# Whole 128x128 array tiles for the first queries' scores, their transposes and the last tokens' values

## The chip, the cores and the metric

One Trainium2 chip, of which the kernel uses one core. The time is the device time of one execution in microseconds (us), as the median of several runs; a profiled execution of the same kernel gives the trace from which all rows below come.

## The reference

Three stages follow each other on 4 sequences of 576 tokens. The first is windowed attention with 8 heads of 64 (each query sees itself and the 63 tokens before it). The second is a mixture of four causal attention experts with 64 channels each, of which each token takes the two with the largest gate. The third multiplies by cosines and sines of a projection, mixes tokens and channels and adds a rectified product. The change touches the second stage alone:

```
logits = x @ w_gate                      # gates: [token, 4]
for e in range(E):                       # E = 4 experts, Hd = 64
    q, k, v = x @ wq[e], x @ wk[e], x @ wv[e]
    scores = scale * (q @ k.transpose(0, 2, 1))
    scores = np.where(causal, -1000000000.0, scores)
    ...
    a /= a.sum(-1, keepdims=True) + 1e-09
    ye = a @ v @ wo[e]
    ...
```

## The kernel before, in words

All matrix products run on TensorE: a weight load puts a stationary operand of up to 128 rows and 128 columns into the array, and a matmul streams the moving operand past it. Where 32-bit precision is wanted, an operand is split into a high and a low part (`mm3`: three matmuls instead of one).

The work of the four images (the four sequences; `b` is 0 to 3) is cut into streams, which generator functions write: `phase_a` (windowed attention, matmuls of lines 288, 316, 156 and 159), `qk` (projections to queries and keys), `vg_gates` (projections to values and gates, four experts' values and the four gate columns side by side, 260 columns), `attn` (expert attention, in two passes `ep` of two experts each, thus 8 passes in all), `wo` (its output), and later `theta`, `mix` and `channel` for the third stage. `merge` interleaves the streams by costs written out by hand (the dictionary `KN`); the attention of one image runs beside the windowed attention and the projections of the next. A planner in the framework then sorts the instructions of each engine by when it estimates them to be ready, and sets the semaphores.

`vg_gates` goes over the tokens in five tiles: four of 128 and a last one of 64 (576 = 4 x 128 + 64). The tokens are the stationary operand, so the last tile loads 64 columns of weights. Line 384 copies the sums from PSUM to SBUF on ScalarE.

`attn` goes over the queries in five tiles of another cut: a first one of 64 queries (`t == 0`, `m = 64`), then four of 128. For each tile and each of the two experts, the scores are one or two pairs of matmuls (lines 460 and 462, queries stationary); VectorE adds the mask and takes the maximum (line 464), ScalarE the exponential (line 469), VectorE sums and inverts (lines 473 and 474), and GpSimd or VectorE scales by sum and gate (line 481). The scaling writes the diagonal block of both experts into the tile `pd`, of which two buffers take turns. TensorE transposes the other blocks (line 492) and the diagonal one (line 498, tile `bdt`); copies bring them back to SBUF (lines 494 to 502), and the products with the values follow (lines 156, 159 and 510), those of lines 156 and 159 in halves of 64 columns of the array, the second half from column 64 on. For the first tile, scores, transposes and copies have 64 queries: the scores load 64 columns of weights, the transpose has 64 rows of weights and an identity matrix of 64x64.

Of the kernel before, what the change touches and what calls it, by code (L numbers as in the profile page):

```python
# [21 lines left out]
P = 128  # L22
# [35 lines left out]
def kernel(ctx, tc, qT, kT, vw, consts, w_in, w_o, w_th, w_tk, w_ch, outT):  # L58
    nc = tc.nc
# [5 lines left out]
    ident, ma1, ma0 = (cst[:, P * i : P * i + P] for i in range(3))  # L65
# [17 lines left out]
    def bank(shape, tag, name):  # L83
        return ps.tile(shape, F32, tag=tag, bufs=BANKS[tag], name=name)

    def pool_mul(out, in_, by):
        nc.gpsimd.tensor_scalar(out=out, in0=in_, scalar1=by, scalar2=1.0,  # L87
                                op0=ALU.mult, op1=ALU.mult)
# [10 lines left out]
    def mm3(out, wh, wl, xh, xl, first, last):  # L99
        nc.tensor.matmul(out, wh, xh, start=first, stop=False)  # L100
        nc.tensor.matmul(out, wh, xl, start=False, stop=False)  # L101
        nc.tensor.matmul(out, wl, xh, start=False, stop=last)  # L102
# [96 lines left out]
    KL = [bp.tile([P, S], F32R, tag=f"KL{e}", name=f"KL{e}") for e in range(E)]  # L199
    for e in range(E):  # L200
        z = slice(64 - 64 * (e % 2), 128 - 64 * (e % 2))
# [172 lines left out]
    def vg_gates(b):  # L374
        xh, xl = X[b]
        vg = bp.tile([P, 5, E * D + E], F32, tag="vg", bufs=2, name=f"vg{b}")
        VG[b] = vg
        for i in range(5):
            w = min(P, S - i * P)
            g = bank([P, E * D + E], ("ggggg", ("as", "ta", "g", "as", "ta"), ("as", "ta", "as", "ta", "as"), ("bs", "tb", "bs", "tb", "bs"), ("bs", "g", "tb", "g", "bs"))[KN["VB"][b]][i], f"vg{b}{i}")  # L380
            for c in range(NC):
                mm3(g[:w], xh[:, c, i * P : i * P + w], xl[:, c, i * P : i * P + w],
                    wih[:, c, 2 * P : W0], wil[:, c, 2 * P : W0], c == 0, c == NC - 1)
            nc.scalar.copy(out=vg[:w, i, :], in_=g[:w])
            yield 1.3

        sh4 = [P, 5, E, E]
        lg = bp.tile([P, 5, E], F32, tag="lg", bufs=2, name=f"lg{b}")
        nc.gpsimd.memset(lg[64:128, 4, :], 0.0)
        pool_mul(lg[:, 0:4, :], vg[:, 0:4, E * D :], 1.0)  # L390
        pool_mul(lg[0:64, 4, :], vg[0:64, 4, E * D :], 1.0)
        mx = bp.tile([P, 5], F32, tag="gmx", name=f"gmx{b}")
        nc.vector.tensor_reduce(out=mx, in_=lg, op=ALU.max, axis=AX.X)
        ex = GX[:, :, :E]
        nc.vector.tensor_sub(out=ex, in0=lg, in1=mx.unsqueeze(2).to_broadcast([P, 5, E]))
        nc.scalar.activation(out=ex, in_=ex, func=AF.Exp)
        lf, lo = lg.unsqueeze(2).to_broadcast(sh4), lg.unsqueeze(3).to_broadcast(sh4)
        df = bp.tile(sh4, F32, tag="gle", name=f"gdf{b}")
        nc.vector.tensor_sub(out=df, in0=lf, in1=lo)
        gt = bp.tile(sh4, F32, tag="ggt", name=f"ggt{b}")  # L400
        nc.vector.scalar_tensor_tensor(out=gt, in0=df, scalar=0.0, in1=tie.unsqueeze(1).to_broadcast(sh4),
                                       op0=ALU.is_equal, op1=ALU.mult)
        nc.vector.scalar_tensor_tensor(out=gt, in0=df, scalar=0.0, in1=gt, op0=ALU.is_gt, op1=ALU.add)
        rk = bp.tile([P, 5, E], F32, tag="grk", name=f"grk{b}")
        nc.vector.tensor_reduce(out=rk, in_=gt, op=ALU.add, axis=AX.X)
        nc.vector.scalar_tensor_tensor(
            out=ex, in0=rk, scalar=1.5, in1=ex, op0=ALU.is_lt, op1=ALU.mult
        )
        sm = bp.tile([P, 5], F32, tag="gsm", name=f"gsm{b}")
        nc.vector.tensor_reduce(out=sm, in_=GX, op=ALU.add, axis=AX.X)  # L410
        nc.vector.reciprocal(out=sm, in_=sm)
        nc.vector.tensor_mul(out=ex, in0=ex, in1=sm.unsqueeze(2).to_broadcast([P, 5, E]))
        gw = bp.tile([P, 5, E], F32, tag="gw", bufs=2, name=f"gw{b}")
        nc.vector.tensor_copy(out=gw[64:128, 1:5, :], in_=ex[0:64, 1:5, :])
        nc.vector.tensor_copy(out=gw[0:64, 1:5, :], in_=ex[64:128, 0:4, :])
        last = nc.vector.tensor_copy(out=gw[0:64, 0, :], in_=ex[0:64, 0, :])
        if b == B - 1:
            gated[0] = last
        GW[b] = gw
# [3 lines left out]
    def sbank(b, shape, name):  # L423
        ns[0] += 1
        return bank(shape, "as" if b == B - 1 and ns[0] % KN["SB"] == 0 else "bs", name)

    def tbank(b, shape, name):
        nt[0] += 1
        return bank(shape, "ta" if b == B - 1 and nt[0] % KN["TB"] == 0 else "tb", name)

    def attn(b, ep):
        vg, gw = VG[b], GW[b]
        for i in range(2):
            e = 2 * ep + i
# [4 lines left out]
        for t in range(5):  # L439
            w = QW[t]  # L440
            q0 = 0 if t == 0 else 64 + P * (t - 1)
            m = 64 if t == 0 else P
# [5 lines left out]
            ss = sums(1, BS)  # L448
            sm = bp.tile([P, 2], F32, tag="bsm", bufs=4, name=f"bsm{b}{ep}{t}")
            pd = bp.tile([P, 2, 64], F32, tag="bpd", bufs=2, name=f"bpd{b}{ep}{t}")  # L450
            for i in range(2):
                e = 2 * ep + i
                n = f"{b}{e}{t}"
                qs, ka = QS[b, e], KA[b, e]
                ms = pn[:, i]
                cuts = [(0, w)] if w <= 512 else [(0, w // 2), (w // 2, w)]
                nm = bp.tile([P, 2], F32, tag="bnm", bufs=6, name=f"bnm{n}")
                for ci, (a, z) in enumerate(cuts):
                    s = sbank(b, [P, 512], f"bs{n}{a}")
                    nc.tensor.matmul(s[:m, : z - a], qs[:, q0 : q0 + m], ka[:, a:z],  # L460
                                     start=True, stop=False)
                    nc.tensor.matmul(s[:m, : z - a], qs[:, q0 : q0 + m], KL[e][:, a:z],  # L462
                                     start=False, stop=True)
                    nc.vector.tensor_tensor_reduce(  # L464
                        out=ms[:m, a:z], in0=s[:m, : z - a], in1=mb[:m, mo + a : mo + z],
                        scale=-0.125, scalar=nm[:m, 0:1] if ci else 3.0e38,
                        op0=ALU.add, op1=ALU.min, accum_out=nm[:m, ci : ci + 1],
                    )
                ex = nc.scalar.activation(out=ms[:m, :w], in_=ms[:m, :w], func=AF.Exp,  # L469
                                     bias=nm[:m, ci : ci + 1], scale=-1.0, accum_out=ss[:m, i, 0:1])  # L470
                if (b, ep, t, i) == (3, 1, KN["LT"], 1):
                    late[0] = ex
# [13 lines left out]
            for j0 in range(0, t, 2):  # L486
                jn = min(2, t - j0)
                pt = tbank(b, [P, 2, 2, P], f"bpt{b}{ep}{t}{j0}")
# [6 lines left out]
                else:  # L495
                    nc.scalar.copy(out=pT[:, j0 : j0 + jn], in_=pt[:, :jn])
            pt = tbank(b, [P, P], f"bdt{b}{ep}{t}")
            nc.tensor.transpose(pt[:, :m], pd[:m].rearrange("p h d -> p (h d)"), ident[:m, :m])
            if KN["BD"][b] == 0 or KN["BD"][b] == 1 and t % 2:
                nc.vector.tensor_copy(out=pT[:, t, 0, :m], in_=pt[:, :m])  # L500
            else:
# [2 lines left out]
            for f in together():  # L504
                for j in reversed(range(t)):
                    for i in range(2):
                        e = 2 * ep + i
# [383 lines left out]
    for i in range(2):  # L891
        nc.gpsimd.memset(VD[i][0:64, :, 1], 0.0)
        nc.gpsimd.memset(VD[i][64:128, :, 0], 0.0)
    merge((KN["QK"][8], qk(0, 0)), (KN["VG"][0], vg_gates(0)), (KN["PA"][6], phase_a(1, range(KN["AS"][1]))),
          (KN["CW"][5], load_w(w_in[:, W0:], NC, lambda c: wih[:, c, W0:], lambda c: wil[:, c, W0:], "bms")))
    for b in range(B):
        todo = [(KN["AT"][2 * b], attn(b, 0)), (KN["QK"][2 * b], qk(b, 1))]
        if KN["WOI"] == 2 * b:
            todo.append((KN["CW"][6], load_w(w_o, 2, lambda c: woh[c], lambda c: wol[c], "zc")))
# [16 lines left out]
        if b == 3:  # L916
# [4 lines left out]
            wkh += [kp.tile([P, S], F32R, name=f"wkh{c}") for c in range(NK0, 9)]  # L921
            wkl += [kp.tile([P, S], F32R, name=f"wkl{c}") for c in range(NK0, 9)]
        todo = [(KN["AT"][2 * b + 1], attn(b, 1))]
        if b < B - 1:
            todo += [(KN["QK"][2 * b + 1], qk(b + 1, 0)), (KN["VG"][b + 1], vg_gates(b + 1))]
# [100 lines left out]
```

## Time and profile before

| | before |
|---|---|
| median of 3 runs | 505.35 us (502.71 to 507.21) |
| profiled execution | 505.36 us |
| its span, first to last instruction | 503.6 us |
| TensorE's mean granted clock | 0.997 |
| busy: TensorE, VectorE, ScalarE, GpSimd | 480.2, 375.3, 343.4, 319.7 us |

In the rows, PE is TensorE's matmuls and PEld its weight loads, DVE is VectorE, ACT is ScalarE, POOL is GpSimd; L498 is line 498 of the kernel. A shape such as 64\*128 ahead of an operand is rows\*columns of the array. A matmul's recorded end is modelled and overlaps the next, so distances between starts say more than durations.

### The profile page before, as it was taken

What the parts mean: (1) busy time and instruction counts of PE and PEld (TensorE: products, weight loads), DVE (VectorE), ACT (ScalarE), POOL (GpSimd) and SP (SyncE); (2) the same over time, 40 slices, a digit from 0 to 9 for tenths busy, and PEclk for the clock granted to TensorE, in tenths of its full rate; (3) what the DMA queues carried; (4) which work ended last, traced back from release to release, by engine and by line L of the source; (5) the groups of instructions that cost most, each with busy time, mean ns of one, the idle gap of its engine ahead of it and who ended that gap; (6) DMA issues with size and microseconds to landing.
All of it is one profiled execution on the core that took longest, in us unless ns stands there. A gap on an engine that the chain in (4) does not pass through costs nothing.

```text
span 503.6 us, 12053 instructions
## 1 busy us (share of the span) xinstructions
PE 480.2 (95%) x4128; PEld 447.6 (89%) x4128; DVE 375.3 (75%) x1268; ACT 343.4 (68%) x1066; POOL 319.7 (63%) x406
## 2 busy tenths in 40 slices
PE   7899989999999999999999899999998999999997
PEld 5788978899998998989878788999998999999997
DVE  5857978776777858846898758987679938894942
ACT  7948778776877977869596698886177627652620
POOL 6758788772764861345595457679658926891770
PEclk9999998999999999999999999999999999999999
DMA  7574242430525242211146944231352044202002
GB/s 271 184 224 135 81 157 87 157 94 7 176 59 184 84 149 94 63 44 53 51 154 218 305 142 163 60 89 42 116 158 64 22 142 130 64 22 96 2 1 95
DMA packets 45614, 55.92 MB, mean 111 GB/s; under 512 B 6640, under 2 KB 34288, under 8 KB 45552
## 3 DMA queue, kind: packets, MB, share of 16 engines
q1 hardware_dynamic: 44688, 52.46, 32.9%
q10 hardware_dynamic: 864, 2.69, 1.6%
q8 instruction: 33, 0.54, 0.4%
q14 instruction: 29, 0.24, 0.2%
HBM read 43.34 MB, written 11.80 MB: 109 GB/s over the span
## 4 chain that ended last, share of the span: by engine, by line
PE 55%; DVE 19%; POOL 8%; ACT 7%; issue 6%; DMA 4%; SPq 0%; POOLq 0%; DVEq 0%; ACTq 0%
PE as L288 4%; PE c L100 3%; PE c L102 3%; PE apt L316 3%; PE c L101 3%; PE qk L100 3%; PE ao L159 2%; PE qk L102 2%; PE qk L101 2%; PE bs L460 2%; PE bpt L492 2%; PE vg L100 2%; ACT bms L469 2%; PE vg L102 2%; PE bs L462 2%
## 5 line engine op out<-in xcount | busy, mean ns | idle before, releaser
L311 POOL TENSOR_TENSOR ams<-ams,arc 128x384 f32<-128x384 f32 x48 | 39.8, 834 | 39.2 <-ACT ams L304 12.9
L304 ACT ACTIVATE ams<-ams,anm 128x128 f32<-128x128 f32 x144 | 56.5, 396 | 5.5 <-DVE anm L296 5.0
L469 ACT ACTIVATE bms<-bms,bnm 64x64 f32<-64x64 f32 (+4 forms) x80 | 44.8, 562 | 19.4 <-DVE bnm L464 17.9
L288 PE MATMUL as<-kt,QD 128*128 128x128 f32 x288 | 42.8, 286 | 2.1 <-DVE arc L309 0.7
L288 PEld LDWEIGHTS as<-kt,QD 128*128 128x128 f32 x288 | 37.1, 196 | 5.4 <-issue 2.0
L464 DVE CUSTOM_DVE_ANT_0 bms<-bs,mb 64x64 f32<-64x64 f32 (+4 forms) x80 | 32.3, 422 | 10.1 <-PE bs L462 6.0
L296 DVE CUSTOM_DVE_ANT_0 ams<-as,cst 128x128 f32<-128x128 f32 x144 | 34.5, 283 | 3.4 <-PE apt L316 2.1
L87 POOL TENSOR_SCALAR QD<-qt 64x576 f32<-64x576 f32 x24 | 31.0, 1290 | 8.6 <-DMA qt<-in_dram 4.1
L481 POOL TENSOR_SCALAR bpd<-bms,bsm,gw 128x64 f32<-128x64 f32 (+1 forms) x47 | 20.5, 437 | 22.9 <-DVE bsm L474 4.9
L97 POOL TENSOR_TENSOR cu<-x2T,cu 128x288 fp32r<-128x288 f32 x32 | 28.9, 916 | 8.0 <-ACT cu L94 8.0
L100 PE MATMUL y<-wkh,z 128*128 128x288 f32 x108 | 32.3, 302 | 0.1
L460 PE MATMUL bs<-KA,QS 128*128 128x288 f32 (+4 forms) x96 | 31.1, 333 | 1.0 <-DVE bnm L464 0.8
L101 PE MATMUL y<-wkl,z 128*128 128x288 f32 x108 | 32.0, 297 | 0.0
L102 PE MATMUL y<-wkh,z 128*128 128x288 f32 x108 | 31.3, 297 | 0.0
L660 ACT ACTIVATE ang<-th,magic 128x256 f32<-128x256 f32 x36 | 16.8, 469 | 20.5 <-PE th L102 20.0
L780 POOL TENSOR_TENSOR x2T<-x2T,u 128x288 f32<-128x288 f32 x20 | 16.6, 841 | 21.3 <-DVE u L791 11.1
L481 POOL TENSOR_SCALAR bms<-bms,bsm,gw 128x384 f32<-128x384 f32 (+3 forms) x40 | 26.7, 667 | 3.0 <-DVE bsm L474 3.0
L668 DVE TENSOR_TENSOR ang<-xk,ang 128x512 f32<-128x512 f32 x32 | 21.6, 683 | 8.8 <-ACT ang L665 5.7
L462 PE MATMUL bs<-KL,QS 128*128 128x288 f32 (+4 forms) x96 | 27.6, 297 | 0.0
L304 ACT ACTIVATION_READ_ACCUMULATOR ams<-ams,anm 128x1 f32 x144 | 27.6, 192 | 0.0
L316 PE MATMUL apt<-cst,ams 128*128 128x128 f32 x144 | 24.4, 277 | 3.3 <-ACT apv L321 2.1
L492 PE MATMUL bpt<-cst,bms 128*128 128x128 f32 x160 | 27.0, 278 | 0.2 <-DVE ol L97 0.2
(337 smaller groups left out, 2033.0 us busy)
## 6 DMA issues: line engine op xcount, KB each, us to landing
vt<-in_dram SPq DMA_DIRECT2D x48, 192.0 KB, 3.0
or<-od SPq DMA_DIRECT2D x32, 256.0 KB, 3.2
kt<-in_dram SPq DMA_DIRECT2D x15, 320.0 KB, 3.1
qt<-in_dram SPq DMA_DIRECT2D x16, 288.0 KB, 3.0
out_dram<-x2T SPq DMA_DIRECT2D x32, 144.0 KB, 1.8
w64k<-in_dram SPq DMA_DIRECT2D x5, 576.0 KB, 3.7
od<-oh SPq DMA_DIRECT2D x8, 288.0 KB, 2.1
od<-ol SPq DMA_DIRECT2D x8, 288.0 KB, 2.5
```

What stands on the lines that cost most here:

```text
L100: nc.tensor.matmul(out, wh, xh, start=first, stop=False)
L101: nc.tensor.matmul(out, wh, xl, start=False, stop=False)
L102: nc.tensor.matmul(out, wl, xh, start=False, stop=last)
L288: nc.tensor.matmul(s[:, i, :], qd[:, blk], kt[:, 64 * blk : 64 * blk + 128], start=True, stop=True)
L304: nc.scalar.activation(out=ms[:, i, :], in_=ms[:, i, :], func=AF.Exp, bias=nm[:, i : i + 1], scale=-1.0, accum_out=sm[:, i, 0:1],)
L311: nc.gpsimd.tensor_mul(out=ms, in0=ms, in1=rc.unsqueeze(2).to_broadcast([P, 3, P]))
L316: nc.tensor.transpose(pt[:, i, :], ms[:, i, :], ident)
L460: nc.tensor.matmul(s[:m, : z - a], qs[:, q0 : q0 + m], ka[:, a:z], start=True, stop=False)
L462: nc.tensor.matmul(s[:m, : z - a], qs[:, q0 : q0 + m], KL[e][:, a:z], start=False, stop=True)
L469: ex = nc.scalar.activation(out=ms[:m, :w], in_=ms[:m, :w], func=AF.Exp, bias=nm[:m, ci : ci + 1], scale=-1.0, accum_out=ss[:m, i, 0:1])
L481: eng.tensor_scalar(out=dst, in0=src, scalar1=sm[:m, i : i + 1], scalar2=gw[:m, t, 2 * ep + i : 2 * ep + i + 1], op0=ALU.mult, op1=ALU.mult)
L492: nc.tensor.transpose(pt[:, jj, i, :], pn[:, i, P * j : P * j + P], ident)
```

## The change

Three places that used a part of the array use all of it. The last tile of values and gates takes the last 128 tokens (64 of them a second time) and keeps the upper 64 partitions of the result. The scores of the first 64 queries load the first 128 queries; only the first 64 rows are read afterwards. The diagonal transpose of the first tile takes all 128 rows of `pd` and a 128x128 identity; rows 64 to 127 of `pd` are set to zero by GpSimd for it, ahead of the scores.

```diff
         for i in range(5):
             w = min(P, S - i * P)
...
+            tok = slice(i * P + w - P, i * P + w)
             for c in range(NC):
-                mm3(g[:w], xh[:, c, i * P : i * P + w], xl[:, c, i * P : i * P + w],
+                mm3(g, xh[:, c, tok], xl[:, c, tok],
                     wih[:, c, 2 * P : W0], wil[:, c, 2 * P : W0], c == 0, c == NC - 1)
-            nc.scalar.copy(out=vg[:w, i, :], in_=g[:w])
+            nc.scalar.copy(out=vg[:w, i, :], in_=g[P - w :])
...
             pd = bp.tile([P, 2, 64], F32, tag="bpd", bufs=2, name=f"bpd{b}{ep}{t}")
+            if m < P:
+                nc.gpsimd.memset(pd[m:], 0.0)
...
-                    nc.tensor.matmul(s[:m, : z - a], qs[:, q0 : q0 + m], ka[:, a:z],
+                    nc.tensor.matmul(s[:, : z - a], qs[:, q0 : q0 + P], ka[:, a:z],
                                      start=True, stop=False)
-                    nc.tensor.matmul(s[:m, : z - a], qs[:, q0 : q0 + m], KL[e][:, a:z],
+                    nc.tensor.matmul(s[:, : z - a], qs[:, q0 : q0 + P], KL[e][:, a:z],
                                      start=False, stop=True)
...
-            nc.tensor.transpose(pt[:, :m], pd[:m].rearrange("p h d -> p (h d)"), ident[:m, :m])
+            nc.tensor.transpose(pt, pd.rearrange("p h d -> p (h d)"), ident)
```

## Rows read from the trace of the kernel before

**Rows 1.** The page: busy time of the engines, and the chain's shares.
```profile
PE 480.2 (95%) x4128; PEld 447.6 (89%) x4128; DVE 375.3 (75%) x1268; ACT 343.4 (68%) x1066; POOL 319.7 (63%) x406
...
PE 55%; DVE 19%; POOL 8%; ACT 7%; issue 6%; DMA 4%; SPq 0%; POOLq 0%; DVEq 0%; ACTq 0%
```

**Rows 2.** Busy time by stage: length, then PE, PEld, DVE, ACT, POOL, clock, DMA.
```profile
45.00:240.00 195.00, 191.63 (x1867) 176.46 (x1866) 143.69 (x684) 151.10 (x544) 119.60 (x181) 0.99 0.31 100
240.00:303.00 63.00, 58.33 (x454) 50.88 (x453) 50.08 (x161) 48.28 (x134) 37.63 (x47) 1.00 0.54 174
```

**Rows 3.** Groups by line and shape, PE: count, busy us, mean ns, idle before.
```profile
L498 PE MATMUL bdt<-cst,bpd 64*128 64x64 f32 x8 | 2.2, 272 | 0.0
```

**Rows 4.** Instructions in order of time, PE, 191.0 to 192.1 us: start, duration.
```profile
191.06 0.31 PE L101 MATMUL x<-ol,woh 128*128 128x320 f32 x1
191.21 0.31 PE L102 MATMUL x<-oh,wol 128*128 128x320 f32 x1
191.45 0.27 PE L498 MATMUL bdt<-cst,bpd 64*128 64x64 f32 x1
191.65 0.40 PE L100 MATMUL qk<-x0h,wih 128*128 128x288 f32 x1
191.89 0.29 PE L101 MATMUL qk<-x0l,wih 128*128 128x288 f32 x1
192.02 0.29 PE L102 MATMUL qk<-x0h,wil 128*128 128x288 f32 x1
```

**Rows 5.** Instructions in order of time, PE, 152.1 to 152.2 us.
```profile
152.09 0.27 PE L498 MATMUL bdt<-cst,bpd 128*128 128x128 f32 x1
152.20 0.28 PE L288 MATMUL as<-kt,QD 128*128 128x128 f32 x1
```

**Rows 6.** The chain that ended last, 125.5 to 126.8 us: start, length.
```profile
125.72 0.59 PE ao L159 x21
126.31 0.20 PE bdt L498
126.51 0.34 PE x L100
```

**Rows 7.** Instructions in order of time, PE, 72.9 to 81.5 us.
```profile
72.94 0.29 PE L462 MATMUL bs<-KL,QS 128*128 128x288 f32 x1
73.07 0.19 PE L460 MATMUL bs<-KA,QS 128*64 128x64 f32 x1
...
81.40 0.27 PE L498 MATMUL bdt<-cst,bpd 128*128 128x128 f32 x1
```

**Rows 8.** Weight loads in order of time, PEld, 113.1 to 113.4 us.
```profile
113.18 0.14 PEld L460 LDWEIGHTS bs<-KA,QS 128*64 128x64 f32 x1
113.24 0.14 PEld L462 LDWEIGHTS bs<-KL,QS 128*64 128x64 f32 x1
113.30 0.19 PEld L288 LDWEIGHTS as<-kt,QD 128*128 128x128 f32 x1
```

**Rows 9.** Weight loads in order of time, PEld, 219.8 to 220.0 us.
```profile
219.80 0.19 PEld L462 LDWEIGHTS bs<-KL,QS 128*128 128x128 f32 x1
219.91 0.19 PEld L460 LDWEIGHTS bs<-KA,QS 128*128 128x128 f32 x1
```

**Rows 10.** Instructions in order of time, PE, 115.4 to 117.0 us.
```profile
115.41 0.28 PE L102 MATMUL vg<-wih,x1l 128*128 128x260 f32 x1
115.53 0.28 PE L100 MATMUL vg<-wih,x1h 128*64 128x260 f32 x1
...
116.94 0.27 PE L510 MATMUL o<-bpT,VD 128*128 128x128 f32 x1
```

**Rows 11.** Groups by line and shape, POOL, two memsets.
```profile
L389 POOL MEMSET lg<- 64x4 f32 x4 | 0.3, 97 | 0.2
L181 POOL MEMSET QD<- 64x192 f32 x1 | 0.3, 253 | 0.1
```

**Rows 12.** Groups by line and shape, ACT, the copies of line 384.
```profile
L384 ACT COPY vg<-vg 64x260 f32<-64x260 f32 x4 | 1.5, 367 | 1.0 <-PE vg L102 1.0
```

## The prediction

> **What bounds the kernel now.** Three views were read in this order: the page's summary and chain of waits, the busy time by stage, and the instructions of the touched places in order of time. The summary shows TensorE busy for 95% of the span, the next engine 75%, and the chain that ended last running over TensorE for 55% of the span, over VectorE for 19% and over GpSimd for 8% [rows 1]. The change lies in the attention stages, which end at about 303 us. From 45 to 240 us TensorE is busy 191.63 of 195.00 us: it hardly waits for anybody, so what it does there sets the pace. From 240 to 303 us, the last of the four images, it is busy 58.33 of 63.00 us and others set the pace for part of the time [rows 2]. A busy TensorE isn't one that works all the time, though: a stall shorter than the recorded tail of a matmul counts as busy. So the third view is read by starts: the time from one start to the next is what an instruction really costs, and the question is at which of the three edited places that distance is longer than it need be.
>
> **The diagonal transposes (8 of 40).** The first query tile has 64 rows, and its transposes use 64 rows of the array [rows 3]. In the example the last matmul ahead of one starts at 191.21 us and should take 0.15 us, as the one before it (191.06 to 191.21); the transpose starts only at 191.45, the next matmul 0.20 us later, and that one takes 0.24 us to its successor where the usual distance is 0.13 [rows 4]. From 191.21 to 192.02 are 0.81 us. A transpose that fills the array has no such gaps: from 152.09 to the next start are 0.11 us [rows 5]. With it the same stretch would be 0.15 + 0.11 + 0.13 + 0.13 = 0.52 us: 0.29 us less, although it streams twice the columns. So TensorE empties itself on the way into a 64-row tile and on the way out. I take six of the eight to be like this. The other two follow directly on the 64-column matmuls of line 159, which make the array empty itself anyway; there I estimate 0.10 us, the excess left on one side (0.24 less 0.13 in [rows 4]). The six of the first three images lie where TensorE sets the pace: 5 x 0.29 + 0.10 = 1.55 us. The two of the last image I count at nothing, because TensorE has 4.67 us of waits in that stage to lose them in. The chain agrees: it runs through five of the eight, 0.20 us each, as at 126.31 us [rows 6].
>
> **The first queries' scores (16 pairs of matmuls).** These load 64 columns of weights and stream 64. On the way in there is no gap: 72.94 to 73.07 us is 0.13, the usual distance of a matmul with 288 columns [rows 7]. Nor is there one within a run or on the way out: the weight loads start 0.06 us apart, and the next full load, of another kind of matmul, 0.06 us after the last of them [rows 8]. So no emptying is saved here. But with so little to stream the load is the limit, and a load of 128 columns for the next tile's scores takes 0.11 us from start to start [rows 9]. The change doubles each load: 0.05 us more. The first load of a pair hides beside the matmul ahead of it (0.13 us), the second doesn't: 12 pairs in the first three images x 0.05 = 0.60 us, and 0.1 us for the place where two pairs follow each other: 0.70 us slower. This part of the change costs time. Its bounds are 0 (all hidden) and 32 x 0.05 = 1.60 us (all bare).
>
> **The last tokens' values and gates (48 matmuls).** They have 64 columns of weights and stream 260. In the run that starts at 115.53 us, 0.12 us after a full-width one at 115.41, twelve of them take until 116.94: 1.41 / 12 = 0.12 us each, and nothing opens at either end [rows 10]. A full load of 0.11 us [rows 9] still fits beside 0.12 us of streaming. I count nothing. The Trainium skill speaks otherwise: its page "TensorEngine Tiling (Array Packing)", section "Key Properties", says that changing the tiling mode drains TensorE. The trace bears this out for the 64-row transposes and not for the 64-column scores and values; what would follow if it held for those is the third rival.
>
> **What is added beside TensorE.** Eight memsets of 64x128 on GpSimd. The nearest rows are 97 ns for 64x4 and 253 ns for 64x192 [rows 11]; I take 0.20 us, 1.6 us in all. GpSimd is busy 119.60 of 195.00 us there [rows 2], so they fit into its idle time as long as the instruction isn't put at a place where it must wait; with GpSimd on 8% of the chain I count 1.6 x 0.08 = 0.13 us. Each whole transpose now also waits for that memset, and all that is queued behind it on TensorE with it; the memset can run before the scores, and a whole softmax lies between them, so the wait ends early. Without that cover it is 8 x 0.20 = 1.6 us. The copies of the last tokens' values now go from the upper half of the partitions to the lower. No row shows ScalarE do this; the four copies take 0.37 us each [rows 12], so the cost lies between nothing and, doubled, 1.5 us. I take nothing, since a copy of the usual kind is the nearest row and the size is unchanged. The vector and scalar instructions on the scores and transposes keep their sizes.
>
> **The sum.** -1.55 + 0.70 + 0 + 0.13 = -0.72 us. The profiled execution took 505.36 us (a span of 503.6 us and 1.8 us around it) and is practically the median, 505.35 us. I predict 504.6 us. By the bounds it lies between 505.36 - 8 x 0.29 = 503.0 (all eight transposes gain in full, the loads hide) and 505.36 + 1.6 + 1.6 + 1.5 = 510.1 us (no emptying saved reaches the end). One per cent, 5.05 us, is about what a measurement of this kernel can tell from no change: three runs of the same kernel spread from 502.71 to 507.21.
>
> **Rivals.**
>
> First, the memset holds GpSimd's queue, and the kernel gets slower. Each engine works off its own list, whose order a planner writes at build time. The memset belongs ahead of the scores, but the buffer that it writes is one of two that turn, and was last read by the transpose of the fourth query tile of the pass before. In the second pass the scores start at 73.07 us, and that transpose only at 81.40 [rows 7]: 8.3 us in which a memset at its written place would keep the softmax scaling, the scaled probabilities of the windowed attention and the query copies waiting behind it. At GpSimd's 61% that is 5.1 us of work pushed back by one such place, and there are three passes of eight where the scores are ahead of that transpose; the other two gaps are about half as long, another 5 us. If the half of these 10 us reaches the end, the time is about 505.4 - 0.7 + 5.1 = 509.8 us, and if it all does, 514.8; it decides once more than some 5.8 us of holding reach the end. Against it: the planner takes what is ready, GpSimd is idle for 39% of the stage, and TensorE has work of other streams to go on with. Chance of over 1%: 0.12.
>
> Second, the new sizes make the planner write another order throughout. The order decides how often TensorE waits, and it waits 3.37 + 4.67 = 8.0 us from 45 to 303 us [rows 2]. A luckier order can win at most these 8.0 us: two thirds of them would give 505.4 - 0.7 - 5.3 = 499.4 us. An unluckier one that adds as much gives 510.0 us. For it: five streams of work compete for every place in the list, so small differences decide. Against it: the changed matmuls are 88 (32 of scores, 48 of values, 8 transposes) of 4128 [rows 1], and gains and losses of single swaps partly cancel. Chance of over 1% faster 0.08, over 1% slower 0.03.
>
> Third, the 64-column matmuls do empty the array, with the gaps hidden in what I took for usual distances. A 64-row transpose loses 0.81 - (0.15 + 0.06 + 0.13 + 0.13) = 0.34 us by it [rows 4], with 0.06 for its own half of the columns. At the 12 pairs of scores and the four images' values, 16 places ahead of 240 us, that would be 5.4 us more: 505.4 - 0.7 - 5.4 = 499.3 us. That is what the page's rule would give. Against it stand the unbroken distances in [rows 7, 8, 10]. Chance: 0.05.
>
> **How the numbers follow.** The forecast, a small gain that a measurement can't tell from none, has 0.72. Faster by over 1%: 0.08 + 0.05 = 0.13. Slower by over 1%: 0.12 + 0.03 = 0.15. The range reaches from 500.5 us, short of the two faster cases' times, to 509.5 us, short of the bound of 510.1 and with the milder half of the first rival; outside remain some 0.1 on each side.
>
> **What would show it.** The eight transposes start 0.11 us before their successor, with no 0.20 us gap around them: the first step holds. Weight loads of the first scores 0.11 us apart in place of 0.06: the second. Values at 0.12 us as before: the third. A memset that starts late with GpSimd idle before it, released by a transpose: the first rival. TensorE's busy time in the stages before 240 us should fall by about 1 us with other waits unchanged; if instead its idle time moves by several us, the order was rewritten and the forecast holds only by luck.

## The result, and the profile after

The changed kernel takes 510.79 us (median of 4 runs, 508.74 to 511.76) beside 504.17 us of the kernel before (median of 4, 502.71 to 507.21): the ratio is 1.0113, with a 95% interval from 1.0078 to 1.0148. A ratio, here and below, compares the fast runs of the two kernels and isn't the quotient of their medians. The changed kernel is slower by 1.1%, where 504.6 us were forecast. The profiled execution took 510.29 us, its span is 508.5 us (503.6 before).

The page after: busy time of the engines, and the shares of the chain that ended last, as in [rows 1].
```profile
PE 480.4 (94%) x4128; PEld 448.3 (88%) x4128; DVE 376.1 (74%) x1268; ACT 346.3 (68%) x1066; POOL 320.0 (63%) x414
...
PE 49%; DVE 21%; ACT 11%; POOL 8%; issue 5%; DMA 5%; SPq 1%; POOLq 0%; DVEq 0%; ACTq 0%
```

No engine has noticeably more to do: TensorE is busy 480.4 us in place of 480.2, and the eight memsets are the 8 new instructions of GpSimd. But the chain has left TensorE: 49% in place of 55%, and ScalarE has 11% in place of 7%. So the time has gone into waits. Where they are is read from the busy time by stage after (columns as in [rows 2]).
```profile
45.00:240.00 195.00, 189.87 (x1867) 175.68 (x1867) 144.74 (x684) 152.35 (x543) 119.29 (x186) 1.00 0.31 100
240.00:303.00 63.00, 56.26 (x419) 49.18 (x418) 49.79 (x159) 46.96 (x127) 37.67 (x49) 0.97 0.55 175
```

In the first stretch TensorE is idle for 195.00 - 189.87 = 5.13 us, before 3.37; in the second 6.74 us, before 4.67 [rows 2]. Together that is 3.8 us more, and the granted clock of the second stretch is 0.97 in place of 1.00. The waits of TensorE from 240 to 310 us name the place: the instructions waited for, us in total, times, longest.
```profile
PE th L100 <- ACT oh L94: 3.3, 1, 3.3
PE th L100 <- DVE ang L664: 1.1, 1, 1.1
PE th L101 <- DVE wot L97: 0.8, 1, 0.8
```

The long one is looked at in order of time, first on TensorE, then on ScalarE for which it waits (start, duration, in brackets the idle time before and what ended it).
```profile
282.43 0.29 PE L465 MATMUL bs<-KL,QS 128*128 128x288 f32 x1
286.06 0.71 PE L100 MATMUL th<-wot,or 128*128 128x256 f32 x2 [3.34 <-ACT oh L94]
```
```profile
278.31 0.38 ACT L505 COPY bpT<-bdt 128x128 f32<-128x128 f32 x2 [2.07 <-PE bdt L501]
281.42 0.74 ACT L127 ACTIVATE wtuk<-w64k 128x576 f32<-128x576 f32 x1 [2.72 <-DMA w64k<-in_dram]
282.06 0.72 ACT L129 ACTIVATE wtuk<-w64k 128x576 uint32<-128x576 uint32 x1
282.69 0.65 ACT L472 ACTIVATE bms<-bms,bnm 128x448 f32<-128x448 f32 x1
...
283.47 0.72 ACT L127 ACTIVATE wtuk<-w64k 128x576 f32<-128x576 f32 x1
...
284.10 0.70 ACT L129 ACTIVATE wtuk<-w64k 128x576 uint32<-128x576 uint32 x1
284.71 1.05 ACT L94 CAST wot<-wot 128x512 fp32r<-128x512 f32 x2
285.65 0.39 ACT L94 CAST oh<-o 128x128 fp32r<-128x128 f32 x2
```

ScalarE stands for 2.72 us on a weight piece of the third stage that is still on its way from memory; the softmax of the attention (line 472) and the casts that TensorE needs (line 94) are queued behind that piece and a second one. None of these instructions is one that the change edits. After the wait the granted clock falls, as the windows around it show: to 0.58 and 0.73, between the two levels of 2.4 GHz (1.00) and 1.2 GHz (0.50), which costs 2.5 x 0.42 + 2.5 x 0.27 = 1.7 us more.
```profile
282.50:285.00 2.50, 0.22 (x2) 0.00 (x0) 2.37 (x5) 2.46 (x6) 1.41 (x2) 1.00 0.88 279
285.00:287.50 2.50, 0.82 (x3) 0.46 (x3) 2.50 (x8) 1.89 (x6) 1.38 (x2) 1.00 0.98 334
287.50:290.00 2.50, 2.34 (x11) 2.34 (x12) 2.50 (x8) 1.43 (x3) 2.50 (x3) 0.58 0.88 297
290.00:292.50 2.50, 2.50 (x17) 2.18 (x16) 1.25 (x5) 1.50 (x4) 1.75 (x2) 0.73 0.60 223
```

So the engines' lists must stand in another order. A count shows that they do. A pass of the attention ends with the end of the tenth matmul `o<-bpT,VD` that belongs to it (line 510 before, 513 after). Up to the eight ends TensorE starts 778, 319, 311, 313, 357, 251, 182 and 165 instructions before, and 775, 311, 324, 301, 368, 257, 192 and 148 after: the count of a pass differs by 3 to 17, though the change adds and removes none on TensorE. Compared place by place in the two traces (by line and tile, the memsets aside), 1220 of TensorE's 4128 places hold another instruction, 512 of VectorE's 1268, 397 of ScalarE's 1066 and 71 of GpSimd's 406; the first of them start at 52 to 58 us.

### The profile page after: what moved, and what is told of

The parts are those of the page before. It is cut to its first block, busy times and chain, and to the rows that moved or that the text cites. A ratio compares the mean times of both kernels' runs of the same rounds, so it can differ in the third digit from the quotient of the medians.

```text
span 508.5 us, 12080 instructions
## 1 busy us (share of the span) xinstructions
PE 480.4 (94%) x4128; PEld 448.3 (88%) x4128; DVE 376.1 (74%) x1268; ACT 346.3 (68%) x1066; POOL 320.0 (63%) x414
## 4 chain that ended last, share of the span: by engine, by line
PE 49%; DVE 21%; ACT 11%; POOL 8%; issue 5%; DMA 5%; SPq 1%; POOLq 0%; DVEq 0%; ACTq 0%
PE as L288 3%; PE c L100 2%; PE c L102 2%; PE qk L100 2%; PE c L101 2%; PE apt L316 2%; DMA wst<-in_dram 2%; PE bs L463 2%; PE bpt L495 2%; PE ao L159 2%; PE qk L101 2%; PE qk L102 2%; DVE ang L671 2%; PE bs L465 2%; PE vg L100 2%
```

## The experiments

Theory "order": the edited instructions cost what the sum says, about nothing, and the new order that the planner writes for the changed kernel costs the 6 to 7 us. Rivals: "instructions" (the whole tiles cost it themselves) and "memset" (the memsets hold GpSimd, the first rival of the prediction). To part order from instructions, the lists of one kernel are forced on another one. Both have the same instructions in the same order of creation apart from the memsets, so a stored list of places can be tied on (the code is shortened):

```diff
+def in_order(tc, nc):
+    for engine, order in stored_lists:        # of PE, DVE, ACT, POOL, SP
+        mine = [i for i in traced if i is on engine and no memset of pd]
+        for a, b in zip(order, order[1:]):
+            tc.add_manual_dep(mine[b], mine[a].name, NoSync, ...)
```

This adds no instruction: every engine's count stays. It tells the planner which one comes first, and the memsets alone stay free. "Old order" is that of the kernel before, "new order" that of the changed kernel.

### One part alone, in the planner's own order

**values_alone**: the last tokens' values and gates in whole tiles, the rest as before.
```diff
+            tok = slice(i * P + w - P, i * P + w)
...
-                mm3(g[:w], xh[:, c, i * P : i * P + w], xl[:, c, i * P : i * P + w],
+                mm3(g, xh[:, c, tok], xl[:, c, tok],
...
+            nc.scalar.copy(out=vg[:w, i, :], in_=g[P - w :])
```


> The kernel before with only the last tokens' values and gates in whole tiles; every engine's order is the old one. The prediction's step: nothing, ratio 1.000. Theory 'every narrow tile empties the array': 4 runs x 0.34 = 1.4 us less, ratio 0.997. Theory 'instructions' by way of the shifted copies: up to 1.5 us more, ratio 1.003.

504.51 us, ratio 1.0012 (0.9982 to 1.0042).

**memsets_alone**: only the eight memsets, the transposes as before.
```diff
+            if m < P:
+                nc.gpsimd.memset(pd[m:], 0.0)
```


> The kernel before plus the eight memsets, whose zeros nobody reads; apart from them every engine's order is the old one. Theory 'order': +0.1 us, ratio 1.000. Theory 'memsets hold GpSimd' (the prediction's first rival): most of the 5.7 us, ratio 1.008 to 1.012, with GpSimd idle ahead of a memset until a transpose of the fourth tile.

504.98 us, ratio 1.001 (0.998 to 1.004). In both traces the lists of TensorE, VectorE, ScalarE and GpSimd hold the same instructions in the same places as before (the memsets aside), and neither kernel costs anything that can be measured. "Memset" falls here.

### The same instructions in the other order

**whole_in_old_order**: the whole change, tied to the old order.
```diff
+    in_order(tc, nc)        # the changed kernel, lists of the kernel before
```


> The whole change, with every engine made to issue its instructions in the order of the kernel before. Theory 'order' (the planner's new order is what costs): the prediction's sum is left, -0.7 us, a ratio of 0.9986, between 0.996 and 1.000. Theory 'instructions' (wider weight loads, memsets, shifted copies cost): the time of the changed kernel stays, ratio 1.011.

**old_matmuls_in_new_order**: the kernel before, with the memsets alone, tied to the new order.
```diff
+    in_order(tc, nc)        # before plus memsets, lists of the changed kernel
```


> TensorE's and ScalarE's operands of the kernel before, with the eight memsets (whose zeros nobody reads here), every engine in the order of the changed kernel. Theory 'order': the loss stays and the 0.7 us that the whole tiles save are missing, +6.4 us, ratio 1.0127, between 1.010 and 1.015. Theory 'instructions': ratio 1.000.

The whole change in the old order takes 502.57 us, ratio 0.9976 (0.9946 to 1.0007). The old matmuls in the new order take 509.48 us, ratio 1.0129 (1.0087 to 1.0171). In their traces the four engines' lists are, place by place, those of the kernel before and those of the changed one. The loss goes with the order and not with the edit; "instructions" falls.

Two controls tie each kernel to its own lists.
```diff
+    in_order(tc, nc)        # before: its own lists; after: its own lists
```


> A control: the kernel before with its own order written out as a list, as in the kernels of the old order. Theory 'order': the list alone changes nothing, ratio 1.000, 504.1 us. Rival: the profiles of most kernels with a written list came to the end of the first pass 2 to 4 us earlier than that of before (86.5 to 87.7 us against 90.4); if the list did that, it is 501.5 us, ratio 0.995, and what was read as the gain of the whole change and of the transposes in the old order falls by as much.

> A control: the changed kernel with its own order written out as a list. Theory 'order': as the changed kernel, ratio 1.011, 509.8 us. Rival 'the list itself gains': 507.3 us, ratio 1.006.

The kernel before with its own lists written out takes 504.88 us, ratio 0.9975 (0.9948 to 1.0003), the changed kernel 511.59 us, ratio 1.0116 (1.0078 to 1.0154). So the list itself gains at most little (the interval reaches from 0.5% to nothing, and by its median the control gains nothing), and the whole change in the old order must be measured against 0.9975: it changes nothing that these runs can tell.

### The two parts with a price, in the old order

**transposes_in_old_order** (with the memsets) and **scores_in_old_order**:
```diff
-            nc.tensor.transpose(pt[:, :m], pd[:m].rearrange("p h d -> p (h d)"), ident[:m, :m])
+            nc.tensor.transpose(pt, pd.rearrange("p h d -> p (h d)"), ident)
```
```diff
-                    nc.tensor.matmul(s[:m, : z - a], qs[:, q0 : q0 + m], ka[:, a:z],
+                    nc.tensor.matmul(s[:, : z - a], qs[:, q0 : q0 + P], ka[:, a:z],
...                                   # and the second matmul of the pair in the same way
```


> Only the eight transposes made whole, with the eight memsets, all in the order of the kernel before. By the prediction's first step, -1.55 us, and +0.13 for the memsets: 503.3 us beside 504.7 us before, ratio 0.997. If the gaps around the 64-row transposes only hide in other waits: ratio 1.000. In the trace each of the eight should start 0.11 us ahead of its successor, with the matmul ahead of it 0.15 us before that.

> Only the first queries' scores with all 128 columns, in the order of the kernel before. By the prediction's second step, +0.70 us: 505.4 us beside 504.7, ratio 1.0014 (bounds 0 and +1.6 us). If the 64-column matmuls emptied the array, this would be a gain of 12 x 0.34 = 4.1 us: ratio 0.992. In the trace the loads of a pair should start 0.11 us apart in place of 0.06.

The transposes: 501.75 us, ratio 0.9943 (0.9919 to 0.9966), which is 0.0032 or 1.6 us below the control with the list alone. The scores: 503.57 us, ratio 0.9998 (0.9971 to 1.0026), 0.0023 or 1.2 us above the control. The control was measured at another time, and each difference is uncertain by some 1.9 us: they have the signs and sizes of the prediction, but neither is clear of nothing. (By medians the scores are even 0.5 us below the kernel before.) The distances between starts in the traces settle it, in the section on the prediction below. transposes_in_old_order has the lowest median of all kernels here and is faster than the kernel before; whether it is faster than that kernel's own lists written out isn't shown.

### Where the new order loses

The planner's lists are cut at what was started at 240 us, where the last image begins.
```diff
+    in_order(tc, nc)        # new lists up to 240 us, the rest in the old order
```


> The whole change. Every engine works off its list in the planner's new order up to what it had started at 240 us in the profile after, and the rest in the order of the kernel before. Theory 'last image': the new order costs most behind 240 us, where TensorE waits for copies that stand behind weight loads on ScalarE: about 504.5 us, ratio 1.000 (502.6 us of the whole change in the old order, and 2 us from the first three images). Theory 'everywhere': the new order's 8 us are spread over the whole attention, three quarters of it ahead of 240 us: 508.5 us, ratio 1.008. Theory 'early' (the 3 us by which the two orders part by 50 us, and nothing later): 505.5 us, ratio 1.002.

```diff
+    in_order(tc, nc)        # old lists up to 240 us, the rest in the new order
```


> The whole change. Every engine's list in the order of the kernel before up to what it had started at 240 us in the profile of before, and the rest in the planner's new order. Theory 'last image': the new order's tail alone brings the loss: about 507.5 to 510 us, ratio 1.006 to 1.012. Theory 'everywhere': 504.7 us, ratio 1.000. Theory 'early': 502.6 us, ratio 0.998.

508.26 us, ratio 1.007 (1.0035 to 1.0104), and 507.74 us, ratio 1.0063 (1.0043 to 1.0083). Either half of the new order costs: "last image" alone falls, "everywhere" alone as well. One profile of each kernel tells more. The table has us from one end of a pass to another, read from TensorE's instructions as above, and TensorE's idle time in them; the last column says what the lists are, up to 240 us and behind.

```
                          pass 1  2 to 5  6 to 8  rest    idle 2-5  6-8   order
before                      90.4   133.6    79.1   200.5     0.8    4.8   old old
values_alone                89.8   133.1    78.7   200.5     0.5    4.4   old old
memsets_alone               91.1   133.2    78.9   200.5     0.6    4.4   old old
before_written_out          88.4   134.1    78.5   200.5     1.2    4.0   old old
whole_in_old_order          87.5   133.5    79.1   200.4     0.9    4.3   old old
transposes_in_old_order     86.5   132.7    78.5   200.5     0.9    5.0   old old
scores_in_old_order         86.8   133.5    79.4   200.4     0.4    3.9   old old
new_order_then_old          90.9   136.9    79.2   200.3     2.8    4.2   new old
old_order_then_new          86.7   134.7    84.1   201.2     2.1    7.2   old new
after                       89.5   134.9    83.1   200.9     2.2    7.3   new new
after_written_out           92.8   135.1    81.3   200.9     2.3    5.6   new new
old_matmuls_in_new_order    87.7   135.5    82.9   201.1     2.6    6.7   new new
```

Passes 6 to 8 take 78.5 to 79.4 us in the old order and 81.3 to 84.1 in the new, whatever the matmuls are. The third stage has 0.4 to 0.9 us more as well where the tail's order is new. In passes 2 to 5 the two orders lie closer: 132.7 to 134.1 us in seven of the eight profiles in the old order, 134.9 to 136.9 in the new. The eighth, old_order_then_new, takes 134.7 in the old order: TensorE waits there once for 1.3 us at 167 us, for a copy on ScalarE, which had itself stood 1.5 us for a weight piece from memory. TensorE's longest wait from 120 to 190 us there:
```profile
PE qk L100 <- ACT vg L385: 1.3, 1, 1.3
```
So a single profile doesn't tell the orders apart in these passes; the run times of new_order_then_old do. The first pass varies from 86.5 to 92.8 us and goes with no order; from 0 to 3.4 us of it are a lower granted clock. That fits the spread of 5 us among the runs of one kernel, of which one profile each was kept.

In passes 2 to 5 the place is at 192 us: TensorE waits 1.0 to 1.6 us there for the score reductions of VectorE (line 467) in all four profiles of the table whose lists are new there, and in none of the others. The windows of the changed kernel and, below, of new_order_then_old show TensorE short of work there, and in the second profile, where it waits half a microsecond longer, the clock falls in the next stretch: 0.34 x 5 = 1.7 us.
```profile
190.00:195.00 5.00, 3.94 (x27) 3.36 (x27) 4.77 (x21) 2.76 (x9) 0.00 (x0) 1.00 0.91 331
195.00:200.00 5.00, 5.00 (x39) 4.89 (x38) 4.84 (x23) 4.22 (x18) 0.00 (x0) 1.00 0.00 0
```
```profile
190.00:195.00 5.00, 3.44 (x26) 3.08 (x24) 4.66 (x21) 2.71 (x8) 1.80 (x4) 1.00 0.55 175
195.00:200.00 5.00, 4.97 (x26) 4.74 (x25) 4.09 (x23) 3.65 (x14) 0.00 (x0) 0.66 0.71 242
```

### What in the new order costs

Three kernels mend a single place of the new order by hand. **new_order_weights_later** takes the weight piece out of the way of the casts at 283 us; the lists are given by the lines of the instructions.
```diff
 ScalarE at 278 us
-127 129 472 127 129 112 94 94 94 94 499
+472 94 94 94 94 127 129 499 127 129 112
 VectorE
-130 136 476 477 484 130 467 467 136 97 467 97 97 97
+476 477 484 97 97 467 467 97 97 130 136 467 130 136
 GpSimd
-138 484 138 484
+484 484 138 138
```


> The whole change in the new order, but at one place of the last image: ScalarE, VectorE and GpSimd do the softmax and the casts of the outputs and of the folded output weights first, and then the conversion of the weights whose load lands at 281 us, on which they stood waiting. Theory 'queue behind a load': TensorE's 3.3 us of waiting at 283 us and the lower clock behind it go: passes 7 and 8 take 49.6 to 50 us in place of 53.1, 506.5 us, ratio 1.0045. Rival 'work that is missing': TensorE has spent its other work and waits anyway, or the later weights delay the third stage as much: 509.8 us, ratio 1.011.

**new_order_two_places** has this, and at 190 us on VectorE:
```diff
-147 415 416 97 417 367 467 484 484 467
+467 467 147 415 416 97 417 367 484 484
```


> As new_order_weights_later, and at 190 us the two reductions of scores on VectorE, whose bank TensorE waits for, ahead of a weight subtraction and the gate copies. Theory 'queue': the 1.0 to 1.6 us of waiting at 192 us go as well, and with them the clock's fall that follows them in some executions: 1 to 2.5 us less than new_order_weights_later, 504 to 505.5 us, ratio 1.000 to 1.0025. Rival: the gates come later and the wait only moves: as new_order_weights_later.

They take 510.78 us, ratio 1.0112 (1.0084 to 1.014), and 510.15 us, ratio 1.01 (1.0067 to 1.0134): no gain, and the theory of a queue behind one load falls as far as its cure goes. The wait of 3.3 us at 283 us is gone, but TensorE's waits from 185 to 310 us of new_order_weights_later show others in its place (the first line's 1.7 us is the place at 192 us, which this kernel leaves alone), and passes 6 to 8 take 83.2 us as before, with 6.6 us idle.
```profile
PE bs L463 <- DVE bnm L467: 1.9, 2, 1.7
PE bpt L495 <- ACT bpT L499: 1.7, 1, 1.7
PE th L100 <- ACT wtuk L127: 1.3, 1, 1.3
PE x L100 <- DVE bnm L467: 1.2, 1, 1.2
```

The clock falls at 290 us instead of 288, as the windows of the same kernel show:
```profile
287.50:290.00 2.50, 1.08 (x9) 0.57 (x8) 2.44 (x5) 1.39 (x4) 1.95 (x2) 1.00 0.96 339
290.00:292.50 2.50, 1.00 (x3) 0.59 (x3) 1.40 (x4) 2.50 (x6) 2.20 (x2) 0.54 0.88 289
292.50:295.00 2.50, 1.98 (x8) 1.58 (x9) 2.50 (x7) 2.31 (x7) 0.08 (x1) 0.50 0.11 41
```

In new_order_two_places the wait at 192 us for the reductions is gone too, and the next matmul, a diagonal transpose, waits 2.0 us for the scaled diagonal blocks: passes 2 to 5 take 137.8 us, 1.7 of them by a lower clock behind that wait. **new_order_gates_first** attacks the same place from the other side, by taking a weight piece from between the gates' steps.
```diff
 VectorE at 184 to 195 us
-130 and 136 ahead of and among 394 to 400, 147 behind 413
+130 and 136 behind 417, 147 behind the second 467 that follows
 GpSimd: 138 behind the next 311; ScalarE: 146 behind the next 472
```


> The whole change in the new order, but the piece of the weights that VectorE converts between the gates' steps at 184 to 190 us (its shift, its merge, and the addition, cast and subtraction that follow on GpSimd, ScalarE and VectorE) stands behind the gates, which then are done 1.2 us sooner. Theory 'VectorE is the bound at this place': the 1.0 to 1.7 us in which TensorE waits at 192 us fall to the 0.4 us of the old order; passes 2 to 5 take 133.5 to 134.5 us in place of 135 to 136.9, the time is 508 to 508.5 us, ratio 1.007. Rival 'the wait only moves', as it did with new_order_two_places: ratio 1.010 to 1.011.

509.3 us, ratio 1.0109 (1.0062 to 1.0156). The wait for the reductions falls from 1.0 to 0.7 us and no further, and passes 2 to 5 take 135.2 us, with 2.2 us idle as before. The windows of this kernel show that wait ahead of 190 us, as its first pass was 2 us shorter.
```profile
185.00:190.00 5.00, 4.27 (x44) 3.97 (x41) 4.62 (x18) 2.04 (x6) 1.98 (x3) 1.00 0.01 3
190.00:195.00 5.00, 4.85 (x31) 4.29 (x32) 4.89 (x24) 4.22 (x16) 0.23 (x1) 1.00 0.98 308
```

The last three ask which engine's list brings the loss behind 240 us. The whole change is in the old order, and behind 240 us the lists of some engines are new.
```diff
+    in_order(tc, nc)        # new behind 240 us: PE, DVE
```


> The whole change in the old order, but behind 240 us the lists of TensorE and VectorE are in the new order (those of ScalarE, GpSimd and SyncE stay old). Passes 6 to 8 take 79 us in the old order and 83 to 84 in the new. Theory 'TensorE spends its other work too early': the matmuls that fold the output weights stand ahead of the attention's outputs in TensorE's new list, so this brings most of the loss: 83 us, ratio 1.006. Rival 'ScalarE's list is what costs': 79 to 80 us, ratio 0.998.

```diff
+    in_order(tc, nc)        # new behind 240 us: PE, DVE, POOL
```


> As tail_tensor_vector, and GpSimd's list new too; only ScalarE's and SyncE's stay old. Theory 'TensorE': as tail_tensor_vector, 83 us for passes 6 to 8. If GpSimd's list is what costs: only this one is slow, ratio 1.006 against 0.998.

```diff
+    in_order(tc, nc)        # new behind 240 us: DVE alone
```


> As tail_tensor_vector with VectorE's list alone new behind 240 us. Theory 'TensorE': 79 us for passes 6 to 8, ratio 0.998. Rival 'VectorE's list, in which weight conversions stand ahead of the softmax': 82 us or more, ratio 1.004.

531.55, 531.0 and 529.03 us, ratios 1.0531 (1.0489 to 1.0573), 1.0531 (1.0484 to 1.0579) and 1.05 (1.0446 to 1.0554). All expectations miss: a list of the new order among lists of the old one costs some 25 us, four times what the whole new order costs. TensorE's waits from 235 to 350 us of tail_vector_alone, where TensorE's own list is the old one:
```profile
PE bdt L501 <- DVE ol L97: 6.0, 4, 2.7
PE bpt L495 <- DVE ol L97: 3.9, 1, 3.9
PE xk L659 <- DVE ang L671: 2.9, 1, 2.9
PE o L156 <- DVE ol L97: 2.2, 1, 2.2
```
Mixed lists cost more than either order and so tell nothing of the engines' shares in the loss; no engine could be named this way.

## Why the prediction was wrong, point by point

**The step that failed** is in the second rival, "the new sizes make the planner write another order throughout": it was given a chance of 0.08 for faster and 0.03 for slower, on the ground that "the changed matmuls are 88 ... of 4128 [rows 1], and gains and losses of single swaps partly cancel". The forecast itself rests on [rows 2] staying as they are. Neither held. The order is rewritten in all eight passes, and it is the whole loss: the same instructions take 0.9976 of before in the old order and 1.0113 in the new, and the old matmuls 1.0129 in the new. The sum put this term at nothing; it measured 6 to 7 us. The rival's sign that would show it was right: TensorE's idle time from 45 to 303 us rose from 8.0 to 11.9 us. That its price came out ("adds as much gives 510.0 us"; 510.79 measured) is partly luck: it is 5.3 us of added waits, where the profile shows 3.8 us of them and 1.7 us of a lower clock, which the prediction doesn't have. Nor do its two chances, the larger one for faster, follow from its own sum, by which a new order can win 8.0 us at most and has no such bound on the other side. That a new order is likelier to lose remains an argument: one was seen. No row ahead of the change said whether the planner would rewrite the order. The values alone and the memsets alone left every list as it was, so the scores, the transposes or the parts together bring it; neither of those two was run in the planner's own order, and which one it is stays open.

**What the loss consists of.** The span grew by 508.5 - 503.6 = 4.9 us between the two profiles: -0.9 in the first pass, which varies by more than that anyway, +1.3 in passes 2 to 5, +4.0 in passes 6 to 8, +0.4 behind them. Of the 5.3 us of passes 2 to 8, 1.4 + 2.5 = 3.9 are idle time of TensorE and 1.7 the lower clock after the wait at 283 us (5.6 against 5.3). The clock fell between 280 and 300 us in the profiles of all seven kernels whose lists of all engines are new there, which cost 1.7 to 3.4 us, and in three of the eight whose lists are old, which cost 1.7. That idle time and clock together are the loss between these two profiles is shown; why this set of lists leaves TensorE more idle was only narrowed: mending one wait or two by hand gained nothing, and taking single engines' lists made it worse. It stays open whether a few swaps together would mend it.

**The transposes (-1.55 us) held.** The example of [rows 4], in whole_in_old_order, in order of time on TensorE:
```profile
188.29 0.31 PE L101 MATMUL x<-ol,woh 128*128 128x320 f32 x1
188.45 0.31 PE L102 MATMUL x<-oh,wol 128*128 128x320 f32 x1
188.59 0.27 PE L501 MATMUL bdt<-cst,bpd 128*128 128x128 f32 x1
188.62 0.38 PE L100 MATMUL qk<-x0h,wih 128*128 128x288 f32 x1
188.84 0.29 PE L101 MATMUL qk<-x0l,wih 128*128 128x288 f32 x1
188.97 0.29 PE L102 MATMUL qk<-x0h,wil 128*128 128x288 f32 x1
```
From the matmul ahead of it to the second one behind its successor are 188.97 - 188.45 = 0.52 us, as predicted, in place of 0.81: 0.29 us less. The same stretch around each of the six transposes of the first three images is 0.29, 0.24, 0.14, 0.29, 0.29 and 0.31 us shorter in the traces of whole_in_old_order and transposes_in_old_order than in that of before: 1.56 us where 1.55 were forecast. The 0.14 is the one behind line 159, for which 0.10 was estimated. The 1.6 us measured against the control agree, but are uncertain by more than that.

**The scores (+0.70 us) held.** The weight loads of the first tile's scores, in order of time in whole_in_old_order, now start 0.11 us apart in place of the 0.06 of [rows 8].
```profile
109.91 0.19 PEld L463 LDWEIGHTS bs<-KA,QS 128*128 128x128 f32 x1 [0.17 <-POOL KA L87]
110.02 0.19 PEld L465 LDWEIGHTS bs<-KL,QS 128*128 128x128 f32 x1
110.13 0.19 PEld L463 LDWEIGHTS bs<-KA,QS 128*128 128x128 f32 x1
110.24 0.19 PEld L465 LDWEIGHTS bs<-KL,QS 128*128 128x128 f32 x1
110.35 0.75 PEld L288 LDWEIGHTS as<-kt,QD 128*128 128x128 f32 x6
```
Around the twelve pairs of the first three images (from the second matmul ahead to the third behind, idle time taken out) TensorE takes 7.6 us in the trace of before, 8.2 in that of scores_in_old_order and 8.3 in that of whole_in_old_order: 0.6 to 0.8 us more. The run time of the scores alone, 1.2 us above the control, is too uncertain to tell 0.70 from either of the prediction's bounds.

**The values (0) and the memsets (+0.13 us) held in their rows.** Their matmuls keep the 0.12 us of [rows 10], here the third group of three of a run in whole_in_old_order, and the copies out of the upper partitions take 0.373 us on average (0.367 in [rows 12]); a memset takes 201 ns, as estimated from [rows 11]. What either costs at the end is too small for the run times (1.0012 and 1.001, each uncertain by 0.3%).
```profile
111.87 0.28 PE L100 MATMUL vg<-wih,x1h 128*128 128x260 f32 x1
111.99 0.28 PE L101 MATMUL vg<-wil,x1h 128*128 128x260 f32 x1
112.11 0.28 PE L102 MATMUL vg<-wih,x1l 128*128 128x260 f32 x1
```
```profile
L385 ACT COPY vg<-vg 64x260 f32<-64x260 f32 x4 | 1.5, 373 | 1.1 <-PE vg L102 1.1
```
```profile
L453 POOL MEMSET bpd<- 64x128 f32 x8 | 1.6, 201 | 1.0 <-PE bdt L501 0.7
```

**The sum (-0.72 us) held within what can be measured**: the whole change in the old order stands at 0.9976 beside 0.9975 of the list alone, 0 us with an uncertainty of 2.1 us.

**The first rival fell.** In whole_in_old_order GpSimd is idle for 1.0 us in all ahead of the eight memsets, 0.7 of it at one that waits for a transpose as was feared, and memsets_alone costs nothing that can be measured. The memset of the second pass starts at 83.5 us, behind the transpose and with no idle time before it.

**The third rival fell.** If the 64-column scores and values emptied the array, whole tiles would have gained 5.4 us, three quarters of it at the scores; neither shows a gain (the intervals leave at most 1.5 us at the scores, 0.9971, and 0.9 at the values, 0.9982). The rule of the Trainium skill's page "TensorEngine Tiling (Array Packing)", section "Key Properties", that changing the tiling mode drains TensorE, agrees here with the 64-row transposes (0.14 to 0.31 us each regained) and not with the 64-column scores and values. It does agree with the 64-column halves of lines 156 and 159, which use all 128 rows too and which the change leaves alone. In the trace of before the first of them starts 0.23 us after the matmul ahead of it, where the usual distance is 0.13:
```profile
147.39 0.29 PE L101 MATMUL qk<-x0l,wih 128*128 128x288 f32 x1
147.52 0.29 PE L102 MATMUL qk<-x0h,wil 128*128 128x288 f32 x1
147.75 0.32 PE L156 MATMUL o<-bpT,vg 128*64 128x128 f32 x1
```
On the way out, a whole transpose or matmul of line 510 starts 0.20 us after the last half of 128 columns, where two whole ones stand 0.11 us apart. So neither the rows nor the columns of a tile alone say whether TensorE empties itself; what does wasn't tried.

## What to carry to other kernels

Where a planner writes the engines' lists from sizes and costs, an edit has two prices: that of its instructions, which the profile gives to a tenth of a microsecond, and that of another order, which it doesn't. Measure them apart by tying the edited kernel to the old lists; here that turns 1.0113 into no change, and the one part that gains, the transposes, into 0.9943, beside 0.9975 for the lists alone. Where run times spread by 1%, the distances between starts at the edited places decide on gains of 1 to 2 us. In a kernel whose bound engine waits for 8 of 258 us, little can be won by a fresh order; the one seen here lost.

## What the runs showed of the hardware that was not expected

- The granted clock of TensorE fell towards half after short single waits. 0.58 and 0.73 followed 3.3 us without a matmul in the changed kernel; 0.66 followed 1.6 us in new_order_then_old, while 1.0 us at the same place in the changed kernel left it at 1.00. The length alone doesn't decide: waits of 1.6 us in old_matmuls_in_new_order and 1.7 us in new_order_weights_later at that place left it at 1.00 too. A wait can cost twice: itself, and some 1.7 us behind it. What decides wasn't tried.
- A diagonal transpose that fills the array took 0.03 us to its successor's start (188.59 to 188.62), less than the 0.11 us of [rows 5], and that successor then took 0.22 us. So the sum over the neighbours, 0.52 us, is the safer measure.
- The first pass took 86.5 to 92.8 us, more than any other stretch varied within one order. Part of it is the clock: it stood at half for a while in the first pass of some profiles and not of others, also of kernels with the same lists (3.4 us lost in memsets_alone, 1.7 in before, none in before_written_out).
